# Rows of 64 bytes instead of 16 in the experts' list in DRAM

## The chip, the core and the metric

The kernel runs on one core of one Trainium2 chip. The metric is the device time of one execution in microseconds (us); less is better. Before the change the median of three runs is 641.91 us (639.21 to 642.95).

## The reference

Attention over 32 packed queries, then attention of all tokens over those 32 packed rows, then a mixture of 8 experts, of which each token takes the one with the largest logit. Cut to what matters:

```python
# q, k, v: 8 batches x 8 heads x 576 tokens x 64; p: 8 x 8 x 32 x 64; all float32
p_packed = sm_attn(p, k, v)                 # softmax attention, scale 1/8
out      = sm_attn(q, p_packed, p_packed)
x        = out with heads side by side       # 4608 tokens x 512
logits = x @ w_gate + modality_bias[modality_id]          # 4608 x 8
e_idx  = argmax(logits);  gate_w = softmax(logits)[e_idx]
for e in range(8):
    mask = e_idx == e
    h = maximum(x[mask] @ w1[e], 0)          # 512 -> 1024
    out[mask] = gate_w[mask] * (h @ w2[e])   # 1024 -> 512
```

## The kernel before

**Attention.** The 8 batches are taken as 4 pairs, each pair in two groups of four heads: 8 units. A unit loads its k, q and v (3.4 MB) through SP's queue (SyncE), makes transposes and scores on PE (TensorE), softmax on ACT (ScalarE) and DVE (VectorE), and writes its part of x to the DRAM tensor `x_scr`. The order of all this on PE, DVE, ACT and SP is written out by hand in the string `ORDER`; a unit begins in ACT's order with two copies `rek<-raw` (line 207), which relay its k.

**Routing.** When both units of a pair are done, `routing` (line 418) works out on DVE and PE for each of the pair's 1152 tokens the expert and the next free row of that expert's list. The lists of all experts lie in one DRAM tensor, `lst`: 8 x 4864 rows. A row holds four 32-bit words: the number of the token, once to gather and once to scatter with, the gate's weight, and an unused one. In SBUF these words stand in `meta`, [128 partitions, 36 columns, 4]. Per pair the queue of POOL (GpSimd) issues nine indirect DMAs (line 467), each of which scatters 128 rows of `meta`, one from each partition, to the rows of `lst` that `dsi` names. There are four such groups, 36 scatters in all. The 256 rows ahead of each expert's list are filled once with a row that points behind the last token, by two DMAs on SP's queue from the tile `pad` (line 99), 1024 rows each.

**Experts.** A slot is a pair of tiles (256 rows) of one expert. `fetch` (line 656) gets a slot's data two slots ahead, all on POOL's queue: one DMA reads 256 rows of `lst` into one of four tiles `mt` (line 657), then two indirect DMAs gather the x of these tokens into `xt` (line 659). PE transposes `xt` (`st_x`, line 672), multiplies with w1 (`st_1`, line 685) and with w2 (`st_2`, line 719), each as three passes over a high and a low part. ACT scales the result with the gate's weight into the only tile `ot` (line 723), and an indirect DMA on POOL's queue scatters it to the output (line 724). The first slots begin while the last pair's attention is still under way; the third and fourth group of scatters therefore fall among the first slots, and POOL's queue is worked off in order: gathers, scatters of rows and scatters of results.

Tables of the slots are made by `table_phase` from counts that stay in SBUF; of `lst` only `fetch` reads.

Of the kernel before, what the change touches and what calls it, by code (L numbers as in the profile page):

```python
# [11 lines left out]
I32 = mybir.dt.int32  # L12
# [6 lines left out]
ds = bass.ds  # L19
# [4 lines left out]
def packed_attn_moe_kernel(  # L24
# [14 lines left out]
    nc = tc.nc  # L39
    B, H, S, D = q.shape  # L40
    J = p.shape[2]
    N, DM = out.shape
# [7 lines left out]
    SCALE = 1.0 / float(D) ** 0.5  # L50
    PAD = 2 * P
    P2 = 2 * P
    R = N + PAD
# [7 lines left out]
    x_scr = dram.tile([N, DM], F32, name="x_scr")  # L61
    lst = dram.tile([E * R, 4], I32, name="lst")

    ident = const.tile([P, P], F32, name="ident")
    make_identity(nc, ident)

# [1 line left out]
    ones_b = const.tile([P, P], BF16, name="ones_b")  # L68
# [17 lines left out]

    meta = const.tile([P, NT, 4], I32, name="meta")
    metaf = meta.bitcast(F32)
    nc.gpsimd.memset(meta, 0)
    pad = const.tile([P, E, 4], I32, name="pad")  # L90
    nc.gpsimd.memset(pad, 0)
# [35 lines left out]

# [1 line left out]
    # phases of the experts: (pairs of batches before it, pairs of tiles that those fill for sure)  # L129
    NA = (NP // 2, NP - 1)  # L130
    SA = [max(0, -((E * (P2 - 1) - m * 2 * S) // P2)) for m in NA]
    NB0 = -(-(N - SA[1] * P2) // P2)            # pairs of tiles after those: at least, at most
    NB1 = (N - SA[1] * P2 + E * (P2 - 1)) // P2
# [4 lines left out]

# [1 line left out]
    wgs = cw.tile([P, KD, E], F32, name="wgs")  # L140
    nc.scalar.dma_start(wgs, w_gate.rearrange("(g p) e -> p g e", p=P))
    # the table of exp is there before it is needed
    warm = sm.tile([P, 1], F32, name="warm", bufs=1)
    nc.vector.memset(warm, 0.0)
    nc.scalar.activation(out=warm, in_=warm, func=AF.Exp)
    # ones where a head (partitions) meets its own half in its pair of heads
    mask = cw.tile([P, 2, D], F32, name="mask")
# [3 lines left out]
    pT = cw.tile([P, 2 * B, P], F32, name="pT")  # L151
    XW = P + E                                  # two heads of x and their share of the logits
    W = dict(raw1=cw.tile([P, KD * F], F32, name="raw1"))
    for z in "hl":
        W["1" + z] = cw.tile([P, KD, F], F32R, name="w1" + z)

    # every head's rows of p transposed into the half of the partitions that is the head's in its pair
    pmask = cw.tile([P, 1, HG, J], F32, name="pmask")
# [20 lines left out]

# [1 line left out]
    # front: steps up to the first softmax and the transposed queries; back: the rest  # L181
    XP = ((0, 3, "a"), (3, 2, "a"), (5, 2, "a"), (7, 2, "a"))    # chunks of x of a step, who brings them out

    def attention(i, g, lt, A, Z):
        # A: pools of the front, Z: pools of the back and of what the back reads
        ps1, ps2 = A["ps1"], A["ps2"]
# [111 lines left out]

        # what the heads' share of the logits is for every row of p
        def gate(u):  # L300
# [101 lines left out]

    # order of the steps' parts in the time of a unit; <: of the unit before it, >: of those behind it
    ORDER = ("x1 e >t0 x3 >t1 x3 x1 >t0 e x3 x2 >>k4 >>k0 >>>dk e >>m1 x2 >t1 >s0 e >>k1 >>k4 x2 >>k0 >e >s0 >>k2 >>k2 "
# [12 lines left out]

# [1 line left out]
    scattered = [[] for _ in range(NP)]  # L419
# [57 lines left out]

# [1 line left out]
    sidx = const.tile([P, 1], F32, name="sidx")  # L479
# [27 lines left out]
    def rotated(e_first):  # L507
        # order of the experts that starts at e_first
        key, m = st_("key"), st_("key_m")
        tsc(out=key, in0=eidx, scalar1=e_first, scalar2=None, op0=ALU.subtract)  # L510
        tsc(out=m, in0=key, scalar1=0.0, scalar2=float(E), op0=ALU.is_lt, op1=ALU.mult)
        tt(out=key, in0=key, in1=m, op=ALU.add)
        return key

    def spans(key, tl):
        # first slot and slot behind the last one of every expert
        bf = sm.tile([P, E, E], F32, name="bf", bufs=1)
        tt(out=bf, in0=key[:, None, :].broadcast_to([P, E, E]), in1=key[:, :, None].broadcast_to([P, E, E]),
           op=ALU.is_lt)
        tt(out=bf, in0=bf, in1=tl[:, None, :].broadcast_to([P, E, E]), op=ALU.mult)  # L520
        starts, ends = st_("starts"), st_("ends")
        nc.vector.tensor_reduce(starts, bf, axis=AX.X, op=ALU.add)  # L522
        tt(out=ends, in0=starts, in1=tl, op=ALU.add)
        return starts, ends
# [19 lines left out]
    def expert_at(starts, ends, v, out_):  # L544
        # expert of slot v (0 when there is none)
        o = sel_at(starts, ends, v, "ex_s")
        m = st_("ex_m")
        tt(out=m, in0=eidx, in1=o, op=ALU.mult)
        nc.vector.tensor_reduce(out_, m, axis=AX.X, op=ALU.add)
        return o  # L550
# [5 lines left out]

    # columns: 0 row of the list, 1 expert, 2 expert of the next segment, 3 expert changes, 4 slot is used,
    # 5 there is a next segment, 6 the first tile of the pair has rows of its own
    def table(key, tl, row_e, tab):
# [11 lines left out]

    # slots of a phase: the rows of the first n batch pairs behind those already used; full pairs of tiles
    # only, or all rows when n_slots is None
    def table_phase(nm, e_first, n, used, n_slots):
# [23 lines left out]
        tt(out=tb[z, 3:4], in0=tb[z, 1:2], in1=e_first[z], op=ALU.not_equal)  # L598
        # expert to have at hand when the phase starts: its first one, or the next when the first is in place
        pr = st_("pref", 1)  # L600
# [6 lines left out]
        if n_slots:  # L607
            used2 = const.tile([P, E], F32, name="used_" + nm)
            tsc(out=used2, in0=starts, scalar1=-1.0, scalar2=float(n_slots), op0=ALU.mult, op1=ALU.add)
            tt(out=used2, in0=used2, in1=tl, op=ALU.min)  # L610
            tsc(out=used2, in0=used2, scalar1=0.0, scalar2=None, op0=ALU.max)
            if used is not None:
                tt(out=used2, in0=used2, in1=used, op=ALU.add)
            le = const.tile([P, 1], F32, name="last_" + nm)
            expert_at(starts, ends, float(n_slots - 1), le)
        else:
            # the last pair of an expert with rows for one tile only
            one = st_("one")
            nc.vector.scalar_tensor_tensor(out=one, in0=tl, scalar=-float(P2), in1=rem, op0=ALU.mult, op1=ALU.add)
            tsc(out=one, in0=one, scalar1=-float(P), scalar2=None, op0=ALU.is_le)  # L620
            tt(out=one, in0=one, in1=sel, op=ALU.mult)
            tsc(out=ends, in0=ends, scalar1=-1.0, scalar2=sidx, op0=ALU.add, op1=ALU.is_equal)
            tt(out=tb[:, 6:7], in0=dot_e(one, ends), in1=tb[:, 4:5], op=ALU.subtract)
            tsc(out=tb[:, 6:7], in0=tb[:, 6:7], scalar1=-1.0, scalar2=None, op0=ALU.mult)
# [8 lines left out]

# [1 line left out]
    def load_w(w, which, e):  # L635
# [19 lines left out]
    def fetch(tb, s, ph, mt, xt):  # L655
        off = val(tb, s, 0, (ET.Pool,), 0, E * R - P2)
        ins = [nc.gpsimd.dma_start(mt, lst[ds(off, P2), :].rearrange("(t p) w -> p t w", p=P))]  # L657
        for t in range(2):
            ins.append(nc.gpsimd.indirect_dma_start(  # L659
                out=xt[:, t], out_offset=None, in_=x_scr[0:NA[ph] * 2 * S] if ph < 2 else x_scr,  # L660
                in_offset=bass.IndirectOffsetOnAxis(ap=mt[:, t, 0:1], axis=0)))
        for z in ins if ph < 2 else ():
            tc.declare_no_dep(ins_of(z), group=("late", "last")[ph], reason="rows of earlier batches only")
        if ph == 1:
            for z in scattered[NA[1] - 1]:
                tc.add_manual_dep(ins_of(ins[0]), z.name, SYNC, reason="rows of the list")
# [26 lines left out]

    # the second tile of the pair only: both parts of its rows side by side
    def st_1_half(M):
# [31 lines left out]

# [1 line left out]
    lts = [sm.tile([P, 2, 2, NC, E], F32, name="lt", bufs=2) for _ in range(NP)]  # L729
# [87 lines left out]

    # weights of the expert of slot n, when they are not those in place; then the next expert's are loaded
    def sw(n, which, after=()):
# [127 lines left out]
```

## Time and profile before

| | |
|---|---|
| timed runs, median (lowest to highest) | 641.91 us (639.21 to 642.95) |
| span of the profiled execution | 658.5 us |
| PE busy in it | 598.8 us, 91% |
| POOL busy in it | 156.2 us, 24% |
| scatters of rows of the list (line 467) | 36, 35.3 us on POOL |
| reads of the list (line 657) | 23, 17.3 us on POOL |

The profile is of one execution; its span goes from the first to the last instruction, and no other time of that execution is given. The span is 16.6 us longer than the median of the timed runs, which are not recorded. Times of single instructions below are of the profiled execution, counted from the span's start. A wait is put down to the instruction that came last by the trace; "issue" stands for time in which the engine waited for nothing that the trace shows, "remote" for a semaphore whose setter it does not show.

### The profile page before, as it was taken

How to read it: one execution, taken by the hardware profiler on the slowest of the kernel's cores; microseconds unless marked ns; L12 is line 12 of the kernel's file. 1: busy time of each engine (PE TensorE's matmuls, PEld its weight loads, DVE VectorE, ACT ScalarE, POOL GpSimd, SP SyncE). 2: the span in 40 equal slices, each digit the busy share in tenths (PEclk: the TensorE clock that was granted, in tenths of full speed). 3: DMA queues.
4: the chain of work that ended last, by engine and by line, in shares of the span. 5: the costliest groups of instructions: out<-in, count | busy, mean ns of one | idle time of the engine just before them, and what ended most of it. 6: DMA issues, size and time to landing. Idle time of an engine off the chain costs nothing. (4 is left out here: it accounts for less than half of the span.)

```text
span 658.5 us, 12203 instructions
## 1 busy us (share of the span) xinstructions
PE 598.8 (91%) x4564; PEld 505.9 (77%) x4564; DVE 261.5 (40%) x670; ACT 238.6 (36%) x457; POOL 156.2 (24%) x204
## 2 busy tenths in 40 slices
PE   3899969868689989999999999999999999999983
PEld 3565646535478968889888988998899899889982
DVE  1488958769955422112612016311120121112181
ACT  4677847756612202121612127221121221222271
POOL 3001050256161171211221322221122112122121
PEclk9999988968779998999999999999999999999998
DMA  9989999934843811111590212720110111112011
GB/s 239 277 200 274 314 303 300 292 92 146 317 148 105 295 30 63 49 49 33 198 397 30 66 50 66 290 66 34 50 49 34 50 50 53 45 50 51 35 50 53
DMA packets 74856, 87.11 MB, mean 132 GB/s; under 512 B 26448, under 2 KB 60240, under 8 KB 74768
## 3 DMA queue, kind: packets, MB, share of 16 engines
q1 hardware_dynamic: 64656, 63.79, 32.6%
q0 software_dynamic: 8528, 21.93, 10.6%
q8 instruction: 47, 0.77, 0.5%
q10 hardware_dynamic: 1584, 0.28, 0.2%
q14 instruction: 41, 0.34, 0.2%
HBM read 66.74 MB, written 19.24 MB: 131 GB/s over the span
## 5 line engine op out<-in xcount | busy, mean ns | idle before, releaser
L685 PE MATMUL ps_h<-x_hl,w1h 128*128 128x256 f32 x1088 | 202.1, 287 | 5.7 <-issue 4.9
L685 PEld LDWEIGHTS ps_h<-x_hl,w1h 128*128 128x128 f32 x1088 | 174.4, 195 | 8.5 <-issue 5.9
L685 PE MATMUL ps_h<-x_hl,w1l 128*128 128x256 f32 x544 | 155.8, 286 | 0.9 <-issue 0.8
L690 DVE SCALAR_TENSOR_TENSOR hl<-ps_h,hh 128x512 fp32r<-128x512 f32 x68 | 46.9, 690 | 263.8 <-ACT hh L689 261.4
L719 PE MATMUL ps_o<-w2h,hh 128*128 128x512 f32 x296 | 118.0, 399 | 2.8 <-ACT ot L723 1.6
L719 PE MATMUL ps_o<-w2h,hl 128*128 128x512 f32 x296 | 116.8, 395 | 0.0
L719 PE MATMUL ps_o<-w2l,hh 128*128 128x512 f32 x296 | 115.8, 391 | 0.3 <-DVEq L844 0.3
L685 PEld LDWEIGHTS ps_h<-x_hl,w1l 128*128 128x128 f32 x544 | 106.1, 195 | 1.5 <-issue 1.4
L689 ACT ACTIVATE hh<-ps_h 128x512 fp32r<-128x512 f32 x68 | 40.6, 597 | 179.0 <-PE ps_h L685 148.0
L724 POOL DMA_INDIRECT out_dram<-ot,mt x37 | 40.5, 1096 | 189.0 <-ACT ot L723 120.7
L723 ACT ACTIVATE ot<-ps_o,mt 128x512 f32<-128x512 f32 x37 | 25.4, 687 | 141.3 <-PE ps_o L719 115.1
L659 POOL DMA_INDIRECT xt<-x_scr,mt x46 | 45.0, 979 | 104.0 <-PE ps_t L672 45.2
L719 PEld LDWEIGHTS ps_o<-w2h,hh 128*128 128x128 f32 x296 | 55.7, 188 | 14.2 <-ACT ot L723 2.5
L719 PEld LDWEIGHTS ps_o<-w2h,hl 128*128 128x128 f32 x296 | 55.6, 188 | 11.6
L719 PEld LDWEIGHTS ps_o<-w2l,hh 128*128 128x128 f32 x296 | 55.7, 188 | 10.9 <-DVEq L844 0.6
L233 ACT COPY kT<-ps 128x384 f32<-128x384 f32 x96 | 44.0, 489 | 37.7 <-PE ps L229 20.4
L467 POOL DMA_INDIRECT lst<-meta,dsi x36 | 35.3, 980 | 83.2 <-DVE starts L522 31.4
L675 DVE TENSOR_TENSOR x_hl<-ps_t,x_hl 128x512 fp32r<-128x512 f32 x42 | 27.5, 683 | 19.7 <-ACTq L844 14.8
L229 PE MATMUL ps<-ident,rek 128*128 128x128 f32 x144 | 25.7, 306 | 10.3 <-POOL meta L114 7.0
L354 PE MATMUL ps<-bd,a2T 64*128 64x136 f32 (+1 forms) x320 | 28.7, 313 | 5.0 <-DVE lt L366 4.7
L657 POOL DMA_DIRECT2D mt<-lst x23 | 17.3, 752 | 61.9 <-DMA out_dram<-ot,mt 48.2
L229 PEld LDWEIGHTS ps<-ident,rek 128*128 128x128 f32 x144 | 17.9, 154 | 17.0 <-POOL meta L114 7.0
(189 smaller groups left out, 706.4 us busy)
## 6 DMA issues: line engine op xcount, KB each, us to landing
raw<-in_moe_w_dram SPq DMA_DIRECT2D x24, 1024.0 KB
raw<-in_k_dram SPq DMA_DIRECT2D x16, 512.0 KB
raw<-in_q_dram SPq DMA_DIRECT2D x16, 512.0 KB
ld_v<-in_v_dram SPq DMA_DIRECT2D x16, 512.0 KB
x_scr<-xs SPq DMA_DIRECT2D x16, 512.0 KB
rek<-in_k_dram SPq DMA_DIRECT2D x16, 64.0 KB
req<-in_q_dram SPq DMA_DIRECT2D x16, 64.0 KB
ld_v<-in_v_dram SPq DMA_DIRECT2D x16, 64.0 KB
```

The lines of the kernel that those rows point to most:

```text
L229: nc.tensor.transpose(out=t[:, c * P:c * P + P], in_=D_[nm + "r"][:, c0 + c, 2 * pr:2 * pr + 2, :], identity=ident)
L233: nc.scalar.copy(out=T_[:, pr, c0 * P:c0 * P + 3 * P], in_=t[:, :3 * P])
L354: nc.tensor.matmul(xp[rows, pr, z * XW:z * XW + XW], a2T[rs, t0:t0 + n], D_["bd", u][rs, :], start=True, stop=True)
L467: ins = ins_of(nc.gpsimd.indirect_dma_start(out=lst, out_offset=bass.IndirectOffsetOnAxis(ap=dsi[:, c:c + 1], axis=0), in_=meta[:, i * NC ...
L659: ins.append(nc.gpsimd.indirect_dma_start(out=xt[:, t], out_offset=None, in_=x_scr[0:NA[ph] * 2 * S] if ph < 2 else x_scr, in_offset=bass. ...
L675: iv = tt(out=M["xl"][:, :, ts], in0=ps, in1=M["xh"][:, :, ts].bitcast(F32), op=ALU.subtract)
L685: nc.tensor.matmul(ps[:, f], M[a][:, j, (f0 + f) * P:(f0 + f) * P + P], M[b][:, j], start=(n == 0), stop=(n == 3 * KD - 1))
L689: ia = nc.scalar.activation(out=M["hh"][:, fs], in_=ps, func=AF.Relu)
L690: iv = nc.vector.scalar_tensor_tensor(out=M["hl"][:, fs], in0=ps, scalar=0.0, in1=M["hh"][:, fs].bitcast(F32), op0=ALU.max, op1=ALU.subtract)
L719: nc.tensor.matmul(op, M[a][:, j, t * P:t * P + P], M[b][:, j, :], start=(n == 0), stop=(n == 3 * KF - 1))
L723: nc.scalar.activation(out=ot, in_=op, func=AF.Copy, scale=mt.bitcast(F32)[:, t, 2:3])
L724: nc.gpsimd.indirect_dma_start(out=out, out_offset=bass.IndirectOffsetOnAxis(ap=mt[:, t, 1:2], axis=0), in_=ot, in_offset=None, bounds_che ...
```

## The change

The row of the list becomes 16 words (64 bytes) wide. `lst`, `meta` and `pad` get the new width, so each scattered row and each row of padding is written as 64 bytes, of which the first 16 are those of before and the rest are the zeros of the memset. `fetch` reads the first 16 bytes of each row, as before, now from rows that lie 64 bytes apart. `meta` takes 2304 instead of 576 bytes of a partition, `pad` 512 instead of 128. (The diff also empties comment lines; they are left out here.)

```diff
     PAD = 2 * P
+    LW = 16
...
-    lst = dram.tile([E * R, 4], I32, name="lst")
+    lst = dram.tile([E * R, LW], I32, name="lst")
...
-    meta = const.tile([P, NT, 4], I32, name="meta")
+    meta = const.tile([P, NT, LW], I32, name="meta")
     metaf = meta.bitcast(F32)
     nc.gpsimd.memset(meta, 0)
-    pad = const.tile([P, E, 4], I32, name="pad")
+    pad = const.tile([P, E, LW], I32, name="pad")
...
-        ins = [nc.gpsimd.dma_start(mt, lst[ds(off, P2), :].rearrange("(t p) w -> p t w", p=P))]
+        ins = [nc.gpsimd.dma_start(mt, lst[ds(off, P2), 0:4].rearrange("(t p) w -> p t w", p=P))]
```

No instruction is added or taken away. On PE, DVE, ACT and SP all stand in the same order with the same waits; on POOL the memset of the padding's second word and one iota beside it, both in the first 4 us, change places.

## Rows read from the trace of the kernel before

**Rows 1.** The page's first part: span; busy time, share and instructions by engine.
```profile
span 658.5 us, 12203 instructions
PE 598.8 (91%) x4564; PEld 505.9 (77%) x4564; DVE 261.5 (40%) x670; ACT 238.6 (36%) x457; POOL 156.2 (24%) x204
```
**Rows 2.** PE's longest waits in 0:82 and in 252:620 (us, times, longest).
```profile
PE ps L229 <- POOL meta L114: 7.0, 1, 7.0
...
PE ps_o L719 <- ACT ot L723: 1.6, 4, 0.4
```
**Rows 3.** POOL in order of time: first scatter of each group, the result's behind the last.
```profile
82.53 1.22 POOL L467 DMA_INDIRECT lst<-meta,dsi  x1 [27.43 <-DVE mxc L535]
...
125.24 0.96 POOL L467 DMA_INDIRECT lst<-meta,dsi  x1 [31.39 <-DVE starts L522]
...
178.43 0.99 POOL L467 DMA_INDIRECT lst<-meta,dsi  x1 [14.34 <-DVE bf L520]
...
233.21 0.99 POOL L467 DMA_INDIRECT lst<-meta,dsi  x1 [0.30 <-issue]
...
245.90 1.01 POOL L724 DMA_INDIRECT out_dram<-ot,mt  x1 [0.30 <-issue]
```
**Rows 4.** PE's waits in 82:97, 125:144, 178:195 and 233:252.
```profile
PE ps L304 <- ACT kT L233: 4.5, 1, 4.5
PE ps L229 <- issue: 1.6, 1, 1.6
...
PE ps L242 <- issue: 6.0, 2, 3.0
PE ps L304 <- ACT kT L233: 2.1, 1, 2.1
...
PE ps_h L685 <- issue: 1.9, 3, 1.1
...
PE ps_h L685 <- issue: 3.9, 4, 1.6
```
**Rows 5.** PE and ACT in order of time behind the fourth group of scatters.
```profile
246.18 0.60 PE L685 MATMUL ps_h<-x_hl,w1h 128*128 128x256 f32 x2 [1.59 <-issue]
...
249.39 0.60 ACT L689 ACTIVATE hh<-ps_h 128x512 fp32r<-128x512 f32 x1 [13.98 <-remote]
```
**Rows 6.** POOL's DMA issues: one line's shortest, median, longest (ns); two lines' groups.
```profile
L467 POOL DMA_INDIRECT lst<-meta,dsi x36: 954/958/1407, 82.5 to 243.3; - x36
...
L659 POOL DMA_INDIRECT xt<-x_scr,mt x46 | 45.0, 979 | 104.0 <-PE ps_t L672 45.2 <-DMA mt<-lst 28.2 <-PE ps_h L685 15.2
L724 POOL DMA_INDIRECT out_dram<-ot,mt x37 | 40.5, 1096 | 189.0 <-ACT ot L723 120.7 <-ACTq L844 53.0 <-ACTq L898 13.8
```
**Rows 7.** SP's issue of the padding; busy time by stretch, last PEclk, DMA share, GB/s.
```profile
41.00 2.68 SPq L99 DMA_DIRECT2D lst<-pad  x2
...
35.00:41.00 6.00, 5.63 (x121) 4.33 (x119) 5.94 (x17) 6.00 (x16) 0.00 (x0) 1.00 1.14 285
...
45.00:48.00 3.00, 3.00 (x24) 1.94 (x26) 1.71 (x5) 1.80 (x5) 0.00 (x0) 1.00 0.32 14
```
**Rows 8.** ACT's copies that begin a unit, around the padding.
```profile
39.09 2.08 ACT L207 COPY rek<-raw 128x1024 f32<-128x1024 f32 x2
...
56.70 1.99 ACT L207 COPY rek<-raw 128x1024 f32<-128x1024 f32 x2
...
75.14 2.07 ACT L207 COPY rek<-raw 128x1024 f32<-128x1024 f32 x2
```
**Rows 9.** First reads of the list, the gathers behind them, their first use on PE.
```profile
154.91 1.56 POOL L657 DMA_DIRECT2D mt<-lst  x2
158.92 1.03 POOL L659 DMA_INDIRECT xt<-x_scr,mt  x1 [2.44 <-DMA mt<-lst]
160.25 1.35 POOL L659 DMA_INDIRECT xt<-x_scr,mt  x1 [0.30 <-issue]
...
172.66 0.55 PE L672 MATMUL ps_t<-ident,xt 128*128 128x128 f32 x3 [0.69 <-DVE run L452]
```

## The prediction

> **What bounds the kernel now.** I read the page's first part, then PE's waits by stretch, then POOL's queue in order of time, then what the DMA engines moved around the padding. PE is busy 91% of the span [rows 1], and where it idles is the question. It is not spread out. Up to 82 us the longest wait is one at the very start; from 252 to 620 us, the long stretch of the experts, the longest item is 1.6 us in four pieces [rows 2]. Between lie the four groups of scatters, which begin at 82.53, 125.24, 178.43 and 233.21 us [rows 3], and every long wait of PE lies in or just behind one of them: 4.5 + 1.6 = 6.1 us, 6.0 + 2.1 = 8.1 us, 1.9 us and 3.9 us [rows 4]. The sum is **20.0 us**. What is odd about them is the cause that the trace gives. Most are "issue", an engine that waits for nothing that is shown; and another engine stands still at the same time without a named setter: ACT for 13.98 us to 249.39 [rows 5]. PE, at that place, does not stop once; the matmuls of line 685 come singly with holes of up to 1.59 us between them [rows 5]. So something that all engines share is slow while small rows are being written to DRAM.
>
> Two readings are open. Either the writes of rows hold the engines up in every run, or they hold up the recording of instructions, which an unprofiled run doesn't do. One number bears on it: the profiled span is 658.5 us [rows 1], the timed median 641.9 us, 16.6 us less, although the time holds all that the span holds and whatever lies around it. So at least 16.6 us of the trace are not in the timed runs, and the only waits in it that are large enough and have no cause in the kernel are these 20.0 us. If they are what the runs lack, 20.0 - 16.6 = **3.4 us** of them at most are left in a timed run. I take this as the likeliest reading, not as shown: the rest of the trace could be stretched instead.
>
> **The change part by part.**
>
> *The scatters' issue.* 36 issues on POOL, median 958 ns [rows 6]. No row of the trace shows a scatter of 64 byte rows. The nearest rows are the gathers and the scatters of results, the same 128 rows to an issue but 2048 bytes each: 979 and 1096 ns on average [rows 6]. With 128 times the bytes an issue costs 0.02 to 0.14 us more; at 4 times I take 0. It would count only in the fourth group, where the nine scatters stand ahead of the result's scatter at 245.90 [rows 3]. Behind that waits ACT's next `ot`, since there is one tile `ot`, and behind ACT waits PE for its `ps_h` to be read out. Bounds there: 9 x 0.14 = 1.2 us more, and a gain of 9 x (958 - 954) ns, that is none.
>
> *The scatters' landing.* A row of 16 bytes shares 64 bytes with three neighbours of its list, which other scatters of the group write; a row of 64 bytes shares with none. If it is the sharing that makes the writes slow, the engines' waits go with it: between 0 and all 20.0 us in the trace, between 0 and 3.4 us in a timed run by the reading above. For the timed run I take the middle, **1.7 us**. What is late next when they go: in the first two groups the units' own loads, in the last two PE's matmuls, which run without holes from 252 us on. For the other side, a loss: the rows bring 4 times the bytes, 36 x 128 x 48 = 221 KB more in all, which at the 285 GB/s of the full stretch [rows 7] is 0.8 us of all DMA engines, spread over four groups beside loads that PE meets two units later. I take 0.
>
> *The padding.* Two DMAs issued from 41.00 to 43.68 us write 2048 rows. Behind them the DMA engines nearly stand: 14 GB/s in 45 to 48 us against 285 GB/s in 35 to 41 us [rows 7]. PE is busy through it (3.00 of 3.00 us), so loads ahead of need hide the hole. What comes through is read from the units: the interval between two units' first copies is 56.70 - 39.09 = 17.61 us before and 75.14 - 56.70 = 18.44 us behind the hole [rows 8], 0.8 us more. Bounds: a gain of 0.8 us when all of the hole goes, up to 3 us, these 45 to 48, if a run without recording had less loaded ahead; a loss of 2048 x 48 = 98 KB at 285 GB/s, 0.3 us. Other small DMAs are issued in the same hole and may be what keeps it open, so I take half: **0.4 us**. The cover is the two units' worth of loaded buffers; without it the whole hole is paid.
>
> *The reads.* 23 DMAs of 256 rows of 16 bytes, as many pieces as before, now from 16 KB instead of 4 KB. The trace has no read with gaps. The tightest place is the first: reads at 154.91, the gather waits 2.44 us for them, the second gather's issue ends at 161.60, and PE transposes from 172.66, after DVE [rows 9]. That leaves 11 us less a landing. Were the wait to double, 2.4 us more would be hidden; a gain is hidden too. Later slots are fetched two slots ahead. Price 0; uncovered it would be 2.4 us, once, since later slots queue behind PE.
>
> *The memsets.* `meta` and `pad` grow four times, on POOL in the first 4 us, long ahead of their use at 41 and 82.53 us. Price 0.
>
> **A rule weighed.** By the rows, waits begin in groups of scatters and up to 3.4 us can be real. The Trainium skill, NOTIFIC — the notification-queue block, section Constraints, capacities, measured rates, says that recording an instruction costs the engine nothing and that the block buffers some 500 records while its writes are slow. By that an engine would stop only some time after writes turned slow, and only in a recorded run; the whole 20.0 us would be the trace's own, and the sum for a timed run 641.9 - 0.4 = 641.5 us. In the fourth group PE stops after eight or more us of scatters, which agrees.
>
> **The sum.** In the trace 658.5 - 20.0 - 0.8 = 637.7 us if all goes. For a timed run 641.9 - 1.7 - 0.4 = **639.8 us**, a gain of 0.3%; between 641.9 (nothing is left to gain) and 641.9 - 3.4 - 0.8 = 637.7 us.
>
> **The rivals.**
>
> *The waits are real.* Then the timed run holds all of them and the 16.6 us lie elsewhere, in every instruction a little. For it: ACT's wait of 13.98 us looks like any other, and the DMA hole of the padding is a hole in data, not in records. Against: no other stretch of the trace looks stretched, and PE's long stretch has next to no waits [rows 2]. The time: 641.9 - 20.0 = 621.9 us if all goes, about 632 us if half does.
>
> *The change doesn't do what it says.* If 64 bytes are as slow to write as 16, the waits stay in the trace and the time stays: 641.9 us. For it: the cost may hang on the number of writes, which is the same. Against: neighbours no longer share. The Trainium skill, DMA: Bandwidth & Descriptors, section Specifications, says that a write of under 512 bytes makes the DMA engine read, modify and write. By that rule 64 bytes are no more whole than 16, and 641.9 us would stand; no row here shows where that limit is.
>
> *Slower: the issue of a scatter grows with its bytes.* The nine scatters of the fourth group hold the result's scatter on POOL, hence `ot`, ACT and PE. The longest issue of the 36 took 1407 ns [rows 6]; nine of these instead of 958 ns are 9 x 0.45 = 4.0 us more, 645.9 us. It is slower by over 0.5% from 3.2 / 9 = 0.36 us an issue. Against it stand the gathers with 2048 bytes.
>
> **How the numbers follow.** What a measurement of this kernel can tell from no change is about 0.5%, 3.2 us: 638.7 to 645.1 us. Forecast 0.42 (one in seven of it beyond 638.7); real waits 0.28; nothing happens 0.18; slower 0.12 (one in twelve of it inside). Faster 0.28 + 0.06 = 0.34, slower 0.11, same 0.55. The range reaches from 630 us, the upper half of the real waits, to 646 us: left out are half of the real waits, 0.14, and less than half of the slower case, 0.05. The forecast's own range is 637.7 to 641.9 us.
>
> **What would show it.** In the trace after: PE's waits in the four groups, 20.0 us now, should nearly go, ACT's 13.98 us with them, and the span should come near 638 us while the time moves by 2. If span and time both fall by 10 us or more, the waits were real. If both stand and the holes are there, width does nothing. If the issue of line 467 is above 1.3 us, the slower case holds. The hole at 45 to 48 us should shorten; if it doesn't, it belongs to the small loads behind the padding. The forecast is wrong above all if the 16.6 us have another source than these waits.

## The result, and the profile after

The changed kernel takes **637.48 us** (median of 11 runs, 633.27 to 640.61) beside 642.42 us for the kernel before (11 runs, 639.21 to 646.05; the record names no chip for either): a ratio of **0.9915**, 95% interval 0.9886 to 0.9943, a gain of 4.9 us. That lies inside the predicted range and on the side called faster, not in the band of 0.5% that was held likeliest. The gain forecast was 2.1 us, and the time lies 0.2 us below the forecast's own range of 637.7 to 641.9 us.

The profiled execution took 637.27 us, and its span is 635.6 us. The page's first part, the answer to [rows 1]:

```profile
span 635.6 us, 12203 instructions
...
PE 588.2 (93%) x4564; PEld 498.8 (78%) x4564; DVE 264.8 (42%) x670; ACT 237.9 (37%) x457; POOL 157.5 (25%) x204
```

PE's longest waits in the four groups of scatters, which now begin at 80.00, 116.51, 164.44 and 215.17 us, the answer to [rows 4] (us, times, longest), one line for each of 95 to 115, 116 to 135, 164 to 180 and 215 to 234 us (80 to 95 us has 0.7 us more), and last PE's longest in 125 to 144 us, the window of [rows 4] for the second group:

```profile
PE ps L355 <- DVE lt L367: 1.3, 1, 1.3
...
PE ps L267 <- ACT a L255: 0.2, 1, 0.2
...
PE ps L355 <- DVE lt L367: 1.7, 1, 1.7
...
PE ps_o L720 <- ACT ot L724: 0.4, 1, 0.4
...
PE ps L355 <- DVE a2T L341: 7.4, 1, 7.4
```

PE's waits without a setter are gone, and so are ACT's of [rows 5]; what ACT keeps in the groups is two "issue" waits of 6.2 us in all ahead of `ot` (3.3 us in the trace of before). New is a wait of 7.4 us for DVE's `a2T`, just behind the second group. The scatters' issue (shortest, median, longest in ns) stands beside [rows 6], the copies that begin a unit beside [rows 8], and the stretches around the padding beside [rows 7] (us, then busy time by engine, PE's granted clock, DMA share, GB/s), the last of them that of the kernel before:

```profile
L468 POOL DMA_INDIRECT lst<-meta,dsi x36: 954/958/1577, 80.0 to 225.3; - x36
```
```profile
38.46 2.08 ACT L208 COPY rek<-raw 128x1024 f32<-128x1024 f32 x2
55.84 2.07 ACT L208 COPY rek<-raw 128x1024 f32<-128x1024 f32 x2
72.60 2.07 ACT L208 COPY rek<-raw 128x1024 f32<-128x1024 f32 x2
90.08 2.07 ACT L208 COPY rek<-raw 128x1024 f32<-128x1024 f32 x2
108.97 2.07 ACT L208 COPY rek<-raw 128x1024 f32<-128x1024 f32 x2
126.75 2.04 ACT L208 COPY rek<-raw 128x1024 f32<-128x1024 f32 x2
```
```profile
45.00:48.00 3.00, 3.00 (x24) 1.60 (x22) 1.77 (x4) 1.74 (x5) 0.32 (x2) 1.00 0.23 10
48.00:51.00 3.00, 3.00 (x23) 1.77 (x23) 2.73 (x5) 1.71 (x4) 2.56 (x6) 1.00 0.80 266
...
48.00:51.00 3.00, 3.00 (x25) 1.62 (x21) 2.27 (x5) 2.07 (x5) 0.00 (x0) 1.00 0.08 6
```

The issue is what it was (958 ns). The hole behind the padding still begins before 45 us but is over by about 48, and the unit behind it takes 72.60 - 55.84 = 16.76 us instead of 18.44. Taken at its word, the comparison of the two traces says that 658.5 - 635.6 = 22.9 us went, while the timed runs say 4.9. The gap between the two numbers is the first thing that the experiments had to settle.

### The profile page after: what moved, and what is told of

The parts are those of the page before. It is cut to its first block, busy times and chain, and to the rows that moved or that the text cites. A ratio compares the mean times of both kernels' runs of the same rounds, so it can differ in the third digit from the quotient of the medians.

```text
span 635.6 us, 12203 instructions
## 1 busy us (share of the span) xinstructions
PE 588.2 (93%) x4564; PEld 498.8 (78%) x4564; DVE 264.8 (42%) x670; ACT 237.9 (37%) x457; POOL 157.5 (25%) x204
## 5 line engine op out<-in xcount | busy, mean ns | idle before, releaser
L686 PE MATMUL ps_h<-x_hl,w1h 128*128 128x256 f32 x1088 | 199.7, 285 | 0.7 <-ACTq L899 0.7
L686 PEld LDWEIGHTS ps_h<-x_hl,w1h 128*128 128x128 f32 x1088 | 172.6, 194 | 2.9 <-ACTq L899 0.9
L676 DVE TENSOR_TENSOR x_hl<-ps_t,x_hl 128x512 fp32r<-128x512 f32 x42 | 27.5, 683 | 19.3 <-ACTq L845 14.4
L355 PEld LDWEIGHTS ps<-bd,a2T 64*128 64x128 f32 (+1 forms) x320 | 20.7, 189 | 18.6 <-DVE a2T L341 8.2
```

The lines of the kernel that those rows point to most:

```text
L355: nc.tensor.matmul(xp[rows, pr, z * XW:z * XW + XW], a2T[rs, t0:t0 + n], D_["bd", u][rs, :], start=True, stop=True)
L676: iv = tt(out=M["xl"][:, :, ts], in0=ps, in1=M["xh"][:, :, ts].bitcast(F32), op=ALU.subtract)
L686: nc.tensor.matmul(ps[:, f], M[a][:, j, (f0 + f) * P:(f0 + f) * P + P], M[b][:, j], start=(n == 0), stop=(n == 3 * KD - 1))
```

## The experiments

Each time below is compared with runs of the kernel before on the same chip. The first eight runs fell on a chip on which the kernel before takes 654 us ("chip A"), the last four on one on which it takes 644.25 us (24 runs, 641.62 to 649.16; "chip B"). This difference between chips turned out to be part of the answer. Gains in us are differences of medians; the ratio on record is not the ratio of the two medians, and the two differ by up to 0.3%.

**The kernel before, unchanged, on chip A.** No edit.

> The kernel before, unchanged, profiled once more. If the waits of PE in the scatter groups are real, each timed run holds them: the profile shows about 20 us of them again, a span near 658 us, and its own time would be near 660 us, which no run of before had (639 to 646). If the runs differ, the span is near 641 us (2 us below the time, as after the change) and PE's waits in the four groups sum to some 3 to 5 us instead of 20. If the recording causes them, span 658 and time 642 stand side by side.

Measured: 654.22 us, ratio 0.9997 (0.9967 to 1.0027). Its profiled execution took 655.24 us with a span of 653.7 us: time and span lie 1.5 us apart, and 1.7 after the change (637.27 and 635.6). The waits of [rows 4] are in it, 17.7 us in the four groups instead of 20.0, and ACT waits 12.3 us in the fourth, where [rows 5] has 13.98, here put down to PE's `ps_h`. PE's waits in 82 to 97 us; ACT in order of time at the same place:

```profile
PE ps L304 <- issue: 4.5, 1, 4.5
PE ps L266 <- ACT kT L233: 1.0, 1, 1.0
```
```profile
94.11 0.48 ACT L233 COPY kT<-ps 128x384 f32<-128x384 f32 x1 [4.51 <-remote]
```

So the waits are in an execution's own time, which lies among the other eleven (651.89 to 658.38 us), and recording doesn't explain 16.6 us. The span of 658.5 us ahead of the prediction lies among those of chip A (647.2 to 658.7 us in the runs of before there) and outside those of chip B (640.0 to 647.5 us): that profile and the timed runs beside it very likely came from chips that differ.

A second profile of the kernel before, beside the runs of the whole change:

> The kernel before, unchanged, one profile on the chip of this call. If before takes 642 us here, PE's waits in the scatter groups should be gone from it (below 5 us instead of 20), which would tell that they are the chip's; if it takes 654 us, they are there again, 15 to 20 us.

Measured: 655.46 us, the same waits (ACT's without a setter 9.6 and 8.9 us), and 19.74 us for the unit behind the padding, 75.93 - 56.19.

**The whole change on chip A.** No edit of the changed kernel.

> The kernel after, unchanged, beside before on one chip. The earlier runs showed that before takes 642 us on one chip and 654 us on another, and that with 654 us PE's waits in the scatter groups stand in the trace though the run is a timed one. If 64 byte rows remove these waits where they occur: about 638 us on a chip where before takes 654, ratio 0.975. If the waits belong to the chip and the change only gains what the two halves gained apart (0.9936 / 0.9983 for the scatters, 0.996 / 0.9983 for the padding, 0.9983 for the pitch): ratio 0.991 to 0.992 on either chip, 649 us where before takes 654, with the waits still in the trace.

Measured: 652.21 us beside 654.72, ratio 0.9956 (0.9930 to 0.9981), which neither expectation named (0.975; 0.991 to 0.992). The waits without a setter are still there. The stretches around the first group (columns as above), and ACT behind it:

```profile
84.00:88.00 4.00, 2.18 (x19) 1.29 (x15) 1.40 (x4) 1.21 (x3) 3.05 (x4) 1.00 0.97 310
88.00:92.00 4.00, 0.39 (x4) 0.30 (x4) 3.07 (x7) 0.77 (x2) 1.74 (x2) 0.67 1.08 376
92.00:96.00 4.00, 3.76 (x44) 3.15 (x44) 1.89 (x6) 3.98 (x11) 0.00 (x0) 0.50 1.12 337
```
```profile
90.26 0.48 ACT L234 COPY kT<-ps 128x384 f32<-128x384 f32 x1 [4.50 <-remote]
```

PE and ACT stand nearly still for about 5 us while the DMA engines go on at 310 and 376 GB/s, with rows of 64 bytes as with rows of 16. These stops go with the chip and not with the rows' width. What went is the padding's: 71.34 - 54.58 = 16.76 us for the unit behind it, where the two profiles of the kernel before on chip A gave 75.28 - 55.67 = 19.61 and 19.74 us.

**The two parts apart, on chip A.** First rows 64 bytes apart, of which padding and scatters write 16; then 64 bytes by the scatters and 16 by the padding; then the reverse.

```diff
-            nc.sync.dma_start(lst.rearrange("(e r) w -> r e w", e=E)[z:z + P], pad)
+            nc.sync.dma_start(lst.rearrange("(e r) w -> r e w", e=E)[z:z + P, :, 0:4], pad[:, :, 0:4])
...
-        nc.vector.tensor_copy(out=dsi, in_=dsf)
+        nc.vector.tensor_scalar(out=dsi, in0=dsf, scalar1=4.0, scalar2=None, op0=ALU.mult)
...
-                out=lst, out_offset=bass.IndirectOffsetOnAxis(ap=dsi[:, c:c + 1], axis=0),
-                in_=meta[:, i * NC + c, :], in_offset=None))
+                out=lst.rearrange("r (q w) -> (r q) w", w=4),
+                out_offset=bass.IndirectOffsetOnAxis(ap=dsi[:, c:c + 1], axis=0),
+                in_=meta[:, i * NC + c, 0:4], in_offset=None))
```

> Rows lie 64 bytes apart as after the change, but padding and scatters write 16 bytes of each only. Theory A (neighbours that share 64 bytes hold each other up): nothing is shared any more, so the time is that after the change, 637.5 us, ratio 0.991. Theory B (a write of less than 64 bytes is slow by itself): the time is that of before, 642.4 us, ratio 1.000, with PE's waits in the groups.

> As after the change, but the padding writes 16 bytes of each 64 byte row; the scatters write 64. If the gain is the scatters': 637.5 us, ratio 0.991, and the hole of the DMA engines at 45 to 48 us is as before (14 GB/s). If the gain is the padding's: 642 us, ratio near 1.000.

> As after the change, but the scatters write 16 bytes of each 64 byte row; the padding writes 64. If the gain is the scatters' by writing whole rows: 642 us, ratio 1.000. If it is the padding's: 637.5 us, ratio 0.991. If half each, 640 us.

Measured: 653.53 us, 0.9983 (0.9957 to 1.0010); 651.48 us, 0.9936 (0.9910 to 0.9963); 652.70 us, 0.9960 (0.9935 to 0.9986). The intervals overlap, so chip A doesn't rank the parts, and by its time the first isn't told from the kernel before. The second doesn't isolate the scatters either: its padding is spaced too, so the hole that was expected with it didn't come. What all three share is clear: the unit behind the padding takes 16.76 to 16.77 us in each, even where only 16 bytes of each 64 are written. For the padding it is enough that a row's neighbours lie elsewhere; that the 64 bytes are written whole is not needed. The stops of the engines are in all three.

**Rows of 32 bytes, on chip A.** `LW = 8` in place of 16, all of it written.

> Rows of 32 bytes, written whole, two to 64 bytes. If sharing 64 bytes is what costs: between, 0.995 to 0.998. If 32 bytes are enough for a whole write: as after, 0.9915.

Measured: 649.65 us, 0.9942 (0.9911 to 0.9974), the unit behind the padding 70.14 - 53.38 = 16.76 us. 32 bytes do what 64 do, as far as chip A can tell; for the padding they do it although two rows share 64 bytes, so it is not the sharing of 64 bytes as such that costs.

**The padding made dearer, on chip A.** The kernel before, with each padding DMA followed by two more of the same form into tensors that nobody reads.

```diff
+    more_lst = [dram.tile([E * R, 4], I32, name=f"lst_more{n}") for n in range(2)]
...
             nc.sync.dma_start(lst.rearrange("(e r) w -> r e w", e=E)[z:z + P], pad)
+            for l2 in more_lst:
+                nc.sync.dma_start(l2.rearrange("(e r) w -> r e w", e=E)[z:z + P], pad)
```

> The kernel before, with the padding written three times: four DMAs more of 1024 rows of 16 bytes, side by side, into two tensors that nothing reads. If the padding of 16 byte rows costs the run some 1.5 us, as the experiments with one half of the change say, two more cost 3 us or more: ratio 1.005 to 1.01. If the hole behind it is hidden by loads ahead: 1.000.

Measured: 663.04 us, 1.0153 (1.0105 to 1.0201), 8.3 us by the medians for two more pairs, about 4 us a pair and more than the 1.005 to 1.01 expected. Its stretches show how the price comes about:

```profile
48.00:51.00 3.00, 3.00 (x23) 1.56 (x24) 2.29 (x5) 2.07 (x5) 0.00 (x0) 1.00 1.03 12
51.00:55.00 4.00, 4.00 (x35) 2.65 (x34) 3.90 (x10) 3.52 (x10) 0.00 (x0) 1.00 0.33 2
55.00:59.00 4.00, 3.43 (x100) 2.61 (x99) 3.88 (x12) 1.94 (x6) 0.00 (x0) 1.00 0.43 72
59.00:63.00 4.00, 0.00 (x0) 0.00 (x0) 0.96 (x3) 0.42 (x1) 2.89 (x7) 0.80 1.08 308
63.00:67.00 4.00, 2.79 (x16) 1.40 (x16) 0.00 (x0) 2.85 (x5) 0.00 (x0) 0.50 0.98 311
```

The DMA engines are first busy with almost no bytes (share 1.03, 12 GB/s) and then idle (0.33, 2 GB/s). PE runs on loaded buffers until 59 us, stands for four, and comes back at a granted clock of 0.50, its lower level of 1.2 GHz.

**Padding alone, on chip B.** The kernel before, its 2048 rows of padding written in one DMA of 128 pieces of 256 bytes; the scatters untouched.

```diff
-    pad = const.tile([P, E, 4], I32, name="pad")
+    pad = const.tile([P, PAD * E // P, 4], I32, name="pad")
...
-        for z in range(0, PAD, P):
-            nc.sync.dma_start(lst.rearrange("(e r) w -> r e w", e=E)[z:z + P], pad)
+        nc.sync.dma_start(lst.rearrange("(e r) w -> e r w", e=E)[:, 0:PAD, :]
+                          .rearrange("e (g n) w -> e g (n w)", n=16), pad.rearrange("p n w -> p (n w)"))
```

> The kernel before with rows of 16 bytes, the scatters unchanged; only the padding's 2048 rows are written in one DMA of 128 pieces of 256 bytes instead of two DMAs of 1024 pieces of 16. Theory: the change's gain is the padding's, which lands slowly in pieces of 16 bytes and holds up the loads queued behind it. Then this alone gives what the change gave in its run beside the kernel before, a ratio of 0.994 to 0.997, the unit's interval behind the padding falls from 18.4 to 19.7 us to about 16.8, and 45 to 48 us moves well over 30 GB/s. Rival: the rows of the scatters carry the gain; then 0.998 to 1.001.

Measured: 642.2 us, **0.9961** (0.9941 to 0.9982), 2.1 us by the medians and 2.5 by the ratio, as the theory asked; the unit behind the padding takes 72.76 - 55.99 = 16.77 us. The same on the changed kernel, pieces of 1 KB:

> The changed kernel with the padding in one DMA of 128 pieces of 1 KB. Theory (the padding's number of small writes is the cost, the scatters' width next to nothing): the same as the kernel with 256 byte pieces beside it, within 0.1%. Rival, that 64 byte scatters gain by themselves: 0.15 to 0.3% below it, 1 to 2 us, seen behind the last of the units. In either case not slower than the changed kernel's 0.9956.

Measured: 636.88 us, **0.9897** (0.9869 to 0.9924). The two differ by 642.2 - 636.88 = 5.3 us, where the theory asked for less than 0.7 us and its rival for 1 to 2 (by the ratios it is 4.1). So the theory, that the padding is all of the gain, fell here, and the rival was still too small.

**Scatters alone, on chip B.** The changed kernel with the wide padding, and beside it the old 2048 rows of 16 bytes into a tensor that nobody reads.

```diff
+    idle = dram.tile([E * R, 4], I32, name="idle")
...
-    pad = const.tile([P, E, LW], I32, name="pad")
+    pad = const.tile([P, PAD * E // P, LW], I32, name="pad")
...
         for z in range(0, PAD, P):
-            nc.sync.dma_start(lst.rearrange("(e r) w -> r e w", e=E)[z:z + P], pad)
+            nc.sync.dma_start(idle.rearrange("(e r) w -> r e w", e=E)[z:z + P], pad[:, 0:E, 0:4])
+        nc.sync.dma_start(lst.rearrange("(e r) w -> e r w", e=E)[:, 0:PAD, :]
+                          .rearrange("e (g n) w -> e g (n w)", n=16), pad.rearrange("p n w -> p (n w)"))
```

> The list with rows of 64 bytes, scatters of 64 bytes, its padding in one DMA of 128 pieces of 1 KB; besides, the 2048 rows of 16 bytes of the kernel before are written at their old place in the queue, into a tensor that nobody reads. The hole is kept, the scatters are those of the changed kernel. Theory: the interval behind the padding is the old one, 18.4 to 19.7 us, and the ratio 0.999 to 1.001, since the scatters' width is worth under 1 us. Rival: the scatters carry it, 0.994 to 0.997.

Measured: 639.24 us, **0.9913** (0.9881 to 0.9945), 5.0 us by the medians and 5.6 by the ratio, although the hole is there: the unit behind the padding takes 76.68 - 55.69 = 20.99 us. The theory's 0.999 to 1.001 missed. On this chip the rows of the scatters are worth 4 to 6 us by themselves.

Where they go is seen in the unit that the first group of scatters falls into. With scatters of 16 bytes (the kernel with the padding alone made wide) it takes 113.59 - 90.24 = 23.35 us. ACT in order of time, the DMA engines and PE by stretch; behind them the longest waits of PE and DVE there:

```profile
90.24 2.07 ACT L207 COPY rek<-raw 128x1024 f32<-128x1024 f32 x2
...
96.30 0.80 ACT L362 COPY xs<-ps 128x768 f32<-128x768 f32 x1 [3.61 <-DMA x_scr<-xs]
...
113.59 2.07 ACT L207 COPY rek<-raw 128x1024 f32<-128x1024 f32 x2
```
```profile
82.00:84.00 2.00, 2.00 (x18) 1.19 (x16) 2.00 (x5) 1.21 (x3) 1.58 (x2) 1.00 0.39 20
```
```profile
90.00:94.00 4.00, 3.73 (x88) 2.43 (x76) 3.33 (x11) 2.69 (x5) 1.59 (x2) 1.00 1.13 257
94.00:98.00 4.00, 0.61 (x4) 0.61 (x6) 0.21 (x1) 1.67 (x3) 0.00 (x0) 0.86 1.12 312
98.00:102.00 4.00, 3.77 (x23) 2.65 (x21) 2.40 (x6) 1.99 (x5) 0.00 (x0) 0.50 1.08 272
102.00:106.00 4.00, 4.00 (x24) 2.02 (x24) 2.46 (x9) 1.34 (x3) 0.00 (x0) 0.79 1.12 307
```
```profile
PE ps L354 <- DVE lt L366: 3.7, 2, 3.5
...
DVE lt L366 <- ACT xs L362: 4.0, 2, 3.7
```

With rows of 64 bytes (the changed kernel's trace of the result, from a chip that, like chip B, has no such stops) the same unit takes 108.97 - 90.08 = 18.89 us, and the same rows read:

```profile
93.32 0.80 ACT L363 COPY xs<-ps 128x768 f32<-128x768 f32 x1 [0.79 <-DMA x_scr<-xs]
```
```profile
82.00:84.00 2.00, 2.00 (x18) 1.12 (x14) 2.00 (x6) 1.07 (x4) 1.43 (x2) 1.00 0.77 180
```
```profile
94.00:98.00 4.00, 2.29 (x23) 1.83 (x23) 1.27 (x5) 2.25 (x7) 0.00 (x0) 1.00 1.14 318
98.00:102.00 4.00, 4.00 (x31) 2.26 (x29) 3.83 (x12) 2.06 (x7) 0.00 (x0) 1.00 1.13 295
```

The scatters of this first group land in 8.4 us (median of the nine) at 16 bytes and in 6.0 us at 64, from the view of their line, the changed kernel last:

```profile
DMA to landing us min/median/max: 3.8/8.4/8.8
```
```profile
DMA to landing us min/median/max: 3.6/6.0/6.5
```

SP issues a load and writes of `x_scr` from 81.6 us on in both kernels; beside the slow scatters they move 20 GB/s in 82 to 84 us, beside the others 180. The write of `x_scr` lands 3 us later, ACT may not refill `xs` until then, DVE waits for ACT's part and PE for DVE. That is 3.61 - 0.79 = 2.8 us of waiting; the remaining 4.46 - 2.8 = 1.7 us of the unit's difference fit PE's granted clock, which after the longer stop is 0.50 and 0.79 over the next eight us instead of 1.00. The other two kernels with 64 byte scatters, on chip B itself, agree: 20.22 us for this unit in the wide kernel with 64 bytes and 18.68 us in the one with the hole, their waits for `x_scr` 1.1 and 0.6 us; and so does the second trace with 16 byte scatters there, of the next experiment: 23.20 us, a wait of 3.0 us, landings of 8.2 us. The two kernels on chip B that have wide padding and differ in the rows' width have spans of 638.6 and 635.1 us, so their traces account for 3.5 us, 3.1 of it in this unit; the medians lie 5.3 us apart, the first kernel's profile being one of its two fastest executions. In the other three groups scatters of 16 bytes cost no more: the unit of the second takes 17.77 us with them and 17.78 us in the changed kernel, and from the last copy of a unit's beginning to the end it is 638.6 - 131.36 = 507.2 us with them and 635.1 - 128.11 = 507.0 us without.

**The padding issued from another queue, on chip B.** The kernel before, `nc.gpsimd` in place of `nc.sync` for the padding's two DMAs.

> The kernel before, with the two padding DMAs of 16 byte rows issued by POOL instead of SP, everything else as before. It tells how the padding holds up the loads. If SP's queue is what stands, because a later load there waits for the padding to have landed, the interval behind it falls to about 16.8 us and the ratio is 0.994 to 0.997. If the 2048 small writes keep the DMA engines themselves busy, the hole in the bytes stays at 45 to 51 us wherever they are issued, and the ratio is 0.999 to 1.001.

Measured: 648.1 us, **1.0056** (1.0031 to 1.0081), slower than either expectation allowed, although the unit at the padding's old place takes 76.74 - 59.97 = 16.77 us. POOL has nothing to wait for and issues them at 4.3 us, so the hole moved to the start, where nothing is loaded ahead:

```profile
L99 POOL DMA_DIRECT2D lst<-pad x2: 929/1017/1105, 4.3 to 5.4; - x2
...
DMA to landing us min/median/max: 9.5/10.5/11.5
```
```profile
12.00:15.00 3.00, 1.70 (x13) 1.31 (x11) 0.00 (x0) 1.63 (x4) 0.00 (x0) 1.00 1.23 148
15.00:18.00 3.00, 0.00 (x0) 0.00 (x0) 0.90 (x2) 0.00 (x0) 0.00 (x0) 0.60 1.12 240
...
12.00:15.00 3.00, 2.68 (x13) 2.28 (x11) 0.98 (x2) 1.72 (x4) 0.00 (x0) 1.00 1.12 297
```

Two small DMAs land in 9.5 to 11.5 us, and with them in flight fully busy DMA engines (1.23) move 148 GB/s, half of the 297 GB/s that the kernel with wide padding moves in the same stretch (the last line). The writes therefore slow the DMA engines themselves. Whether SP's queue standing behind them adds to it, as the idle DMA engines late in the hole suggest, this run doesn't tell, since it changed the moment as well as the queue.

## Why the prediction was right in its range and wrong in its steps

*What recording adds.* "So at least 16.6 us of the trace are not in the timed runs" is the step that failed. It set a time from one set of executions against a span from another. Time and span lie 1.5 to 1.7 us apart in every profiled run, so the gap says nothing of recording. The other executions of the changed kernel and of the experiments have a span on record too, at the same distance, so that the timed runs "are not recorded" isn't borne out, and what recording itself costs no run here shows. The Trainium skill, NOTIFIC — the notification-queue block, section Constraints, capacities, measured rates, says that recording an instruction costs the engine nothing; the waits need no cause in the recording, since they are in the profiled execution's own 655.24 us on chip A.

*The waits of [rows 4], 1.7 us of the sum.* Right that rows of 64 bytes were worth something in the groups of scatters, wrong about what. The 20.0 us don't go with the change: they stand in the changed kernel on chip A, and the kernels with 16 byte scatters on chip B don't have them. They explain most of the difference between the two traces: the unit of the second group takes 146.44 - 117.71 = 28.73 us in the trace of before, 140.90 - 112.53 = 28.37 us with the whole change on chip A, and 131.36 - 113.59 = 17.77 us with 16 byte scatters on chip B. These 11 us are not all a gain, for without the stops PE waits 7.4 us for DVE's `a2T` in the next unit. Counted up to the `a2T` matmuls behind that wait (at 167.55 us before, 153.32 after) the second group costs 49.84 - 44.35 = 5.5 us more in the trace before than in the one after, the stretch from the third group's first scatter to the fourth's 54.78 - 50.73 = 4.1 us, and the rest from there 425.29 - 420.43 = 4.9 us: 14.4 of the 22.9 us. "PE's waits should nearly go, the span near 638" came true in the trace after for a reason that has nothing to do with the change, so that agreement is luck.

*The scatters' landing.* The true term wasn't in the sum: a write of `x_scr` that lands late behind the scatters, ACT's `xs`, and PE's clock behind that, 4 to 6 us on chip B. The trace of before couldn't show it. There PE stands for some 4 us in just that group, for another reason, and by then `x_scr` has landed. The reading of the neighbours was off as well: `routing` counts rows by column and within a column by partition, so the rows that share 64 bytes are mostly those of one scatter, not of others in the group. The list of what is queued beside the scatters (SP's writes and who waits for their tiles) would have named it as a bound; the prediction put the gain at "between 0 and 3.4 us" from the engines' waits alone.

*The padding, 0.4 us.* The mechanism was right, loads ahead of need use up in the hole and what comes through lengthens the unit behind it; the size was short by five to six times: 2.1 us by the medians and 2.5 by the ratio on chip B. Two causes. The interval before the hole, 17.61 us, was taken as the undisturbed one; the unit behind the hole takes 16.76 us without it. And the price of a wait is more than its length: in the first profile of the kernel before on chip A PE's granted clock falls to 0.86 and 0.71 after the hole. In the trace of [rows 8], with the same longest wait of 1.1 us (PE for DVE's `lt`), it stayed at 1.00, which fits that unit's 18.44 instead of 19.61 us. The stretches on chip A, then those of the trace of before:

```profile
59.00:63.00 4.00, 2.77 (x22) 2.12 (x23) 1.63 (x6) 2.03 (x6) 0.00 (x0) 0.86 1.06 300
63.00:67.00 4.00, 4.00 (x24) 2.20 (x24) 2.49 (x9) 1.56 (x5) 0.00 (x0) 0.71 1.11 306
...
59.00:63.00 4.00, 2.67 (x25) 1.62 (x26) 2.44 (x9) 2.49 (x6) 0.00 (x0) 1.00 1.05 313
63.00:67.00 4.00, 4.00 (x34) 2.67 (x36) 2.87 (x9) 2.13 (x6) 0.00 (x0) 1.00 1.14 281
```

Halving the term because other small DMAs share the hole was wrong too: with wide padding and the same small loads the gain is whole. The test named for it, that the hole at 45 to 48 us shortens, was met only at its end (10 GB/s there, then 266 instead of 6).

*Terms at nothing.* The scatters' issue stayed at 958 ns, so the slower rival had no ground. The reads held: the first gather waits 1.94 us for them instead of 2.44, with PE's first use 12.8 us later. The memsets show nowhere. The 319 KB of further bytes are not seen either.

*The range.* The sum held 1.7 us of waits that the change doesn't remove, and lacked the scatters' 4 to 6 us and most of the padding's. The time lies in the range because that reached down to 630 us for the rival of real waits, whose gain did not come; so it is in part luck.

*The rivals.* "The waits are real" was right in its premise, since they are in the time, and wrong in its promise. "The change doesn't do what it says" holds for those waits and for nothing else. The rule of the Trainium skill, DMA: Bandwidth & Descriptors, section Specifications, that a write under 512 bytes is read, modified and written, did not decide it: 16 and 64 bytes both lie under it, yet the first group's scatters land in 8.4 and 6.0 us, and the padding in 256 byte pieces gave 16.77 us for its unit, the same as 64 byte rows.

*What stays open.* Why engines stop without a setter on one chip and not on the other, with the same kernels; on chip A the stops hide the gain of the scatters (23.67 us for the first group's unit before, 98.95 - 75.28, and 95.14 - 71.34 = 23.80 after), which fits that the change gives 2.5 us there and 4.9 us in the result. Whether the scatters, like the padding, need only the spacing and not whole 64 byte writes was tried on chip A alone, where the time can't show it. The transfers beside them say that spacing is enough: in the two us from 0.5 us behind SP's issue of its load in the first group, the DMA engines move 17 to 48 GB/s in five traces with 16 byte rows side by side, and 123 to 202 in the eight with rows 32 or 64 bytes apart; the two kernels that write 16 of each 64 bytes stand at 172 and 123. The trace of before, 256 GB/s there, is the exception; its unit loads were still moving 308 GB/s in the two us ahead. And whether the wide padding beats the change as made: 0.9897 and 0.9915 come from different runs and their intervals overlap.

## What to carry to other kernels

Compare a profile's span with the time of that same execution before reading anything from the gap to a median: a span that doesn't fit the timed runs may come from another chip. Rows of 16 bytes written side by side can cost more than their issue shows, here in the padding and in one group of four, so look at what else is in flight when they land, whose tile that transfer holds, and what PE's clock does after the wait. And take the undisturbed length of a stage from the stage that is really undisturbed, not from the one just before.

## What the runs showed of the hardware

2048 rows of 16 bytes, 32 KB, took 9.5 to 11.5 us to land beside other loads and halved what the DMA engines moved meanwhile; a third and a second copy of them cost about 4 us each. The scatters of the first group, with other transfers started among them, landed in 8.2 and 8.4 us with 16 byte rows side by side (medians of two kernels) and in 6.0 to 6.8 us with 64 byte rows (of three), with four times the bytes; those of the second group in 5.4 and 6.4 us against 5.5 to 6.3, no faster. Two chips differ by 654 to 644 us on the same kernel; on the slower one PE and ACT, and DVE for a part, stand for some us in the groups of scatters while transfers go on, which between the first profile of the kernel before there and that of the wide padding on the other makes 3.0, 4.3 and 5.3 us from the second group on. A wait of PE of about 3.5 us was followed by granted clocks of 0.50 and 0.79 over the next eight us, one of 1.3 us by 1.00 in the changed kernel's trace, and one of 1.1 us by 0.71 in a profile of the kernel before.
